# First attention of a fused kernel: block sums placed by one engine, keys and queries copied by ScalarE, the last two pairs' sums together, channel folds in another order

## The chip, the cores and the metric

One core of one Trainium2 chip runs the whole kernel. The metric is the device time of one execution in microseconds (us); lower is better. All data is float32 (the expert weights arrive as float64 and are converted on the chip).

## The reference

An attention with a local window and one summary key per block, then a Fourier mixing of tokens and channels with a two-layer network behind it.

```python
# attention: 4 batches, 8 heads, 768 tokens, head size 64; block 32, window 16
k_sum = k.reshape(B, H, nb, block, D).max(axis=3)
v_sum = v.reshape(B, H, nb, block, D).mean(axis=3)
scores_l = scale * q @ k.T          # kept where |i - j| < 16
scores_s = scale * q @ k_sum.T + log(block)
a = softmax(concat(scores_l masked, scores_s))
x = a @ concat(v, v_sum)            # heads side by side: (4, 768, 512)
# mixing and network
u = x + real(fft(fft(x, axis=1), axis=2))
un = (u - mean) / sqrt(var + 1e-6)
out = u + relu(un @ w_ch1) @ w_ch2  # 512 -> 2048 -> 512
```

## The kernel before

The batches run one behind the other: attention of the next batch beside the network of this one. Batch 0's attention stands alone at the start (`first_attention`); its order on TensorE (PE), VectorE (DVE) and ScalarE (ACT) is the order in which the code is written (`tc.manual_schedule`). All later instructions are placed by a scheduler, which also answers to code that changes ahead of them. SyncE issues the loads in program order, through eight completion lanes in turn.

The eight heads of batch 0 go as four pairs, g = 0 to 3. For a pair:

- `turn` transposes queries and keys on PE into PSUM (`qk`), four tiles a pair: keys or queries (n = 1 or 0), first or second head (e). `place` copies such a tile with two copies of 64x384 into `kt` or `qt` (L738). `key_maxima` takes the block maxima of the keys into `km` (L692, DVE).
- The scores come in two halves of the tokens: `wide_scores` (PE, L750 with the keys and L754 with the block maxima), `exponentials` (ACT, L759, one a head), `masks` (DVE, a product with `wide`, two a half).
- `add_parts` sums the pair's values by blocks on PE (L773, three parts in a group) into a PSUM bank `vs`, and ACT copies the sums to `words` (L776). `spread_sums` sends them through another matmul (L782), one a head, into the same bank; two copies then write them into rows 96 to 127 of the pair's values tile `vw` (L784): head 0 by DVE, head 1 by ACT, each 32x768.
- `wide_values` multiplies scores and values (PE, L792); DVE divides by the sums and writes the output block into `x`.

Round g works on pair g + 1's scores, places pair g's sums, turns pair g + 2's keys and queries, and ends with pair g's values. In the last round (n == NP) the last pair's own sums are made between its two halves of scores.

Behind each pair's values DVE folds tokens (`fold_sequence`: sums and differences of the two token halves, into `early`, the name `wide` in the profile), a pair's 128 channels at a time. Behind the attention `fold_halves` and `fold_ends` fold the channels into `fold`, for the two parities `par`. ACT writes some edge columns there (L985, L988, L992).

Then the scheduler's part begins: `add_later_blocks(1, 0)` (DVE sums of batch 1's values `vb`), the scaling of the loaded `half` into `vs` (L1822), the conversion of the weights (`convert`: L1145, L1158, L1161, L1163 on DVE, L1146 and L1159 on ACT), and the mixing (`gen_fourier`): matmuls `y` (L1307, L1311), ACT copies of them to `big` (L1312, L1313), matmuls `mx` (L1346, L1348), whose result DVE adds to `x`. Then come the normalisation and the first hidden layer (L1430).

Of the kernel before, what the change touches and what calls it, by code (L numbers as in the profile page):

```python
# [16 lines left out]
P = 128  # L17
# [479 lines left out]
def _main_program(ctx, tc, q, k, v, moe_w_ch1, moe_w_ch2, out):  # L497


    nc = tc.nc  # L500
    B, H, S, D = q.shape
# [79 lines left out]
    def tt(out, in0, in1, op):  # L581
        return nc.vector.tensor_tensor(out=out, in0=in0, in1=in1, op=op).ins  # L582
# [70 lines left out]
    def wide_vw(g):  # L653
        return (vw_bufs + [third, vw_bufs[0]])[g].rearrange("p (e n) d -> p e n d", e=2)
# [85 lines left out]
    def score_banks(g, half):  # L740
        return [abank([P, S2], f"sc_0_{g}_{half}_{e}") for e in range(2)]
# [14 lines left out]
    def exponentials(p, half, banks):  # L756
        n0, n1 = NQ // 2 * half, NQ // 2 * (half + 1)
        for e in range(2):
            nc.scalar.activation(out=p[:, e, n0:n1], in_=banks[e][:, 0:S2].rearrange("p (n c) -> p n c", c=QB), func=AF.Exp,  # L759
                                 scale=SC)  # L760

    def masks(p, half):
        n0, n1 = NQ // 2 * half, NQ // 2 * (half + 1)
        for e in range(2):
            tt(p[:, e, n0:n1], p[:, e, n0:n1], wide[:, None, :].to_broadcast([P, NQ // 2, QB]), ALU.mult)

    def add_parts(g):

        both = bank([P, 2, 2, D], f"vs_0_{g}")
        vw, ps = wide_vw(g), both[:, 0]  # L770
        for i in range(3):
            for c in range(4):
                nc.tensor.matmul(ps[32 * c:32 * (c + 1)], blk[0:WK, i], vw[0:WK, :, 3 * c + i, 0:D],  # L773
                                 start=i == 0, stop=i == 2)
        sums_of = words[:, 4096 + 2 * D * g:4096 + 2 * D * (g + 1)].rearrange("p (e d) -> p e d", e=2)
        nc.scalar.copy(out=sums_of, in_=ps)  # L776
        return sums_of, [both[WK - 32 * e:P - 32 * e, 1, 0] for e in range(2)]

    def spread_sums(g, sums_of, ps):

        for e in range(2):
            nc.tensor.matmul(ps[e], blk[:, 3], sums_of[:, e], start=True, stop=True)  # L782
        for e in range(2):
            (nc.scalar.copy if e else nc.vector.tensor_copy)(  # L784
                out=wide_vw(g)[WK:P, e, :, 0:D], in_=ps[e][:, None].to_broadcast([P - WK, NQ, D]))

    def wide_values(b, g, p, x):
        vw = wide_vw(g)
# [77 lines left out]
    def first_attention():  # L866

        x = x_of[0] = bpool.tile([P, NST, DM], FP, tag="x", bufs=2, name="x_0")
        fold = bpool.tile([P, 7, 2, S2], FP, tag="u", name="fold_0").rearrange("p a k n -> p (a k n)")
        wt["fold"] = split_fold(0, fold)  # L870
        turned = turned_to(0)
        for n in (1, 0):
            for e in range(2):
                turn(0, turned[0], n, e)
        for n in (1, 0):
            place(turned, n, 0, nc.scalar.copy)
            place(turned, n, 1, nc.vector.tensor_copy)
        key_maxima(0)
        load(0, 2)
        load_values(0, 1)  # L880
        load(0, 3)
        load_values(0, 2)
        ps, spread = {}, {}
        for g in range(-1, NP - 1):
            a, n = g + 1, g + 2
            first, second = score_banks(a, 0), None
# [19 lines left out]
            if n < NP:  # L906
                turn(n, turned[0], 0, 1)
                if g < 0:
                    place(turned, 0, 0, nc.scalar.copy)
                place(turned, 0, 1, nc.vector.tensor_copy)  # L910
            exponentials(ps[a], 1, second)
            if n < NP and g >= 0:
                place(turned, 0, 0, nc.scalar.copy)
            masks(ps[a], 1)
# [21 lines left out]
        keep_busy(3, ps[NP - 1][:, 0].rearrange("p n c -> p (n c)"))  # L936
        for par in range(2):
# [7 lines left out]
    def fold_sequence(par, g):  # L945

        x, c = x_of[0], slice(P * g, P * (g + 1))
        tt(early[par][:, :, c], x[:, 0:HT, c], x[:, HT:NST, c], SUB if par else ADD)

    def fold_halves(par, g):  # L950

        sd, zw = early[par], wt["fold"][:, par]
        lo, hi = slice(P * g, P * (g + 1)), slice(HD + P * g, HD + P * (g + 1))
        tt(zw[:, :, lo], sd[:, :, lo], sd[:, :, hi], ADD)
        tt(zw[:, :, hi], sd[:, :, lo], sd[:, :, hi], SUB)

    zqs, fgs = {}, {}

# [857 lines left out]
    weights = gen_weights()  # L1816
    with tc.manual_schedule(engines={mybir.EngineType.PE, mybir.EngineType.DVE, mybir.EngineType.Activation}):
        first_attention()
    add_later_blocks(1, 0)
    with tc.issue_after(marks["fold", 0]):  # L1820
        nc.vector.memset(vs, 0.0)
        nc.vector.tensor_scalar(out=vs[:, :, D], in0=half_of, scalar1=float(BLOCK), scalar2=None, op0=ALU.mult)  # L1822

# [92 lines left out]
```

## Time and profile before

| | us |
|---|---|
| median of 3 runs | 798.8 (797.18 to 800.85) |
| the profiled execution | 798.54 |
| its span, first to last instruction | 796.7 |
| PE busy, share of the span | 773.2, 97% |
| DVE busy | 539.1, 68% |
| ACT busy | 246.4, 31% |
| GpSimd busy | 75.1, 9% |

Shares are means over stages with different limits. The chain that ended last is 84% PE, 10% DVE and 4% ACT over the whole span, yet in the first 110 us it changes engine nearly every microsecond, so that stage is read instruction by instruction. In a timeline row stand the start, the duration, the engine, the line, the operation with what it writes and reads, the shape, the number of merged instructions, and in brackets the engine's idle time before it with what ended it. In a row of windows stand the window, then busy time and instructions of PE, its weight loads, DVE, ACT and POOL, the granted TensorE clock, the share of the DMA engines' time and GB/s.

### The profile page before, as it was taken

The numbers are of one execution on the slowest core, as the hardware profiler recorded it, in microseconds if no ns is written. First come the engines' busy times: TensorE is split into PE (matmuls) and PEld (weight loads), VectorE is DVE, ScalarE is ACT, GpSimd is POOL, SyncE is SP. The second block draws the span as 40 slices with busy tenths as digits, with TensorE's granted clock in tenths as the row PEclk, the third lists the DMA queues.
The fourth block names the chain that finished last, engine by engine and source line by source line (L and its number), as shares of the span: only waits on it lengthen the run. The fifth ranks groups of instructions, "written<-read, shape, count | busy, mean of one in ns | idle before, by whom it ended". The sixth has DMA issues, their size and how long they took to land.

```text
span 796.7 us, 14870 instructions
## 1 busy us (share of the span) xinstructions
PE 773.2 (97%) x6028; PEld 581.4 (73%) x6028; DVE 539.1 (68%) x1125; ACT 246.4 (31%) x573; POOL 75.1 (9%) x100
## 2 busy tenths in 40 slices
PE   8899979999999999999999999999999999999997
PEld 5578535545569876688669875688659889889986
DVE  4689999676878838564476726574376887756762
ACT  4545746524635212200126211310125214203300
POOL 0000000000000002200130002300040004201500
PEclk9989999999999999999999999999999999999999
DMA  9997598694774258995344049820614035204001
GB/s 192 262 238 154 133 303 219 213 297 129 212 214 140 78 159 182 254 174 133 119 179 156 31 144 210 218 97 27 250 46 154 29 123 209 93 1 185 1 28 56
DMA packets 135900, 120.35 MB, mean 151 GB/s; under 512 B 94512, under 2 KB 117392, under 8 KB 135824
## 3 DMA queue, kind: packets, MB, share of 16 engines
q1 hardware_dynamic: 134672, 117.05, 53.6%
q0 software_dynamic: 576, 2.10, 0.7%
q8 instruction: 49, 0.80, 0.5%
q10 hardware_dynamic: 576, 0.17, 0.1%
q14 instruction: 27, 0.22, 0.1%
HBM read 95.71 MB, written 23.59 MB: 150 GB/s over the span
## 4 chain that ended last, share of the span: by engine, by line
PE 84%; DVE 10%; ACT 4%; DMA 1%; issue 1%; POOL 0%; SPq 0%; DVEq 0%; ACTq 0%; POOLq 0%
PE ox L1723 17%; PE hx L1430 13%; PE oz L1723 9%; PE hz L1430 7%; PE o L1700 5%; PE oy L1723 4%; PE t L1603 4%; PE hy L1430 4%; PE y L1307 3%; PE f L1603 2%; PE mx L1266 2%; PE sc L808 2%; PE av L844 1%; PE av L849 1%; PE g L1603 1%
## 5 line engine op out<-in xcount | busy, mean ns | idle before, releaser
L1430 PE MATMUL hx<-u,w 128*128 128x384 f32 x384 | 141.1, 495 | 3.3 <-ACT h L1447 1.9
L1430 PEld LDWEIGHTS hx<-u,w 128*128 128x128 f32 x384 | 71.2, 191 | 57.5 <-ACT h L1447 4.4
L1723 PE MATMUL oz<-w,s 128*128 128x256 f32 x336 | 81.7, 380 | 0.0
L1723 PE MATMUL ox<-w,s 128*128 128x256 f32 x336 | 80.1, 380 | 0.0
L1723 PE MATMUL ox<-w,h 128*128 128x256 f32 x336 | 79.6, 381 | 0.0
L1723 PEld LDWEIGHTS ox<-w,h 128*128 128x128 f32 x336 | 63.0, 190 | 10.7 <-issue 1.2
L1430 PE MATMUL hz<-u,w 128*128 128x384 f32 x192 | 70.3, 489 | 0.5 <-DVE u L582 0.5
L582 DVE TENSOR_TENSOR x<-ox,x 128x256 f32<-128x256 f32 x84 | 35.5, 423 | 51.2 <-PE ox L1723 50.8
L1723 PEld LDWEIGHTS oz<-w,s 128*128 128x128 f32 x336 | 63.3, 190 | 8.9 <-DVE x L582 0.4
L1723 PEld LDWEIGHTS ox<-w,s 128*128 128x128 f32 x336 | 63.0, 190 | 9.2 <-DVE x L582 0.3
L1430 PEld LDWEIGHTS hz<-u,w 128*128 128x128 f32 x192 | 36.1, 190 | 26.5 <-DVE u L582 1.1
L1441 ACT COPY h<-hx 128x384 f32<-128x384 f32 x24 | 11.5, 478 | 123.1 <-PE hx L1430 123.1
L1700 PE MATMUL o<-w,h 128*128 128x512 f32 x96 | 41.9, 594 | 0.0
L1723 PE MATMUL oy<-w,h 128*128 128x256 f32 x168 | 40.6, 381 | 0.7 <-ACT h L1652 0.7
L1606 ACT COPY f<-t 128x192 f32<-128x192 f32 x52 | 15.8, 303 | 78.3 <-PE t L1603 78.1
L1582 POOL TENSOR_SCALAR h<-h 128x768 f32<-128x768 f32 x12 | 25.4, 2128 | 137.5 <-DVE h L1562 137.5
L585 POOL TENSOR_TENSOR vb<-vb 96x512 f32<-96x512 f32 (+2 forms) x20 | 20.7, 1037 | 179.0 <-DMA vb<-in_v_dram 112.6
L1430 PE MATMUL hy<-u,w 128*128 128x384 f32 x96 | 36.1, 496 | 0.9 <-DVE h L582 0.9
L1723 PEld LDWEIGHTS oy<-w,h 128*128 128x128 f32 x168 | 31.5, 190 | 5.9 <-ACT h L1652 1.5
L582 DVE TENSOR_TENSOR x<-oz,x 128x256 f32<-128x256 f32 x42 | 17.8, 423 | 26.7 <-PE oz L1723 26.4
L1700 PEld LDWEIGHTS o<-w,h 128*128 128x128 f32 x96 | 18.1, 190 | 22.5 <-issue 22.2
L1460 ACT ACTIVATE h<-hx 128x384 f32<-128x384 f32 x24 | 11.7, 489 | 62.7 <-PE hx L1430 62.7
(234 smaller groups left out, 1337.9 us busy)
## 6 DMA issues: line engine op xcount, KB each, us to landing
w<-dw SPq DMA_DIRECT2D x42, 896.0 KB, 5.9
words<-in_moe_w_ch_dram SPq DMA_DIRECT2D x32, 512.0 KB, 5.7
dw<-w SPq DMA_DIRECT2D x12, 896.0 KB, 6.9
vw<-in_v_dram SPq DMA_DIRECT2D x47, 192.0 KB, 6.1
out_dram<-x SPq DMA_DIRECT2D x23, 256.0 KB, 2.0
vb<-in_v_dram SPq DMA_DIRECT2D x24, 192.0 KB, 7.2
kn<-in_k_dram SPq DMA_DIRECT2D x9, 384.0 KB, 4.5
qn<-in_q_dram SPq DMA_DIRECT2D x9, 384.0 KB, 5.2
```

Of the source, the lines that this page charges most:

```text
L582: return nc.vector.tensor_tensor(out=out, in0=in0, in1=in1, op=op).ins
L585: return nc.gpsimd.tensor_tensor(out=out, in0=in0, in1=in1, op=op).ins
L808: ins = nc.tensor.matmul(ps[h][r:r + 64, i, :], kt[rows, o:o + 64], qt[rows, o:o + BLOCK], start=True, stop=True)
L1266: nc.tensor.matmul(out, y[:, g], table, start=False, stop=True, skip_group_check=True)
L1307: nc.tensor.matmul(y, fgs[b][par][:, st, P * g:P * (g + 1)], fs[par][:, g % 2, st, :], start=(st == 0), stop=(st == n - 1))
L1430: ins = nc.tensor.matmul(ps, w[:, a, kk, :], u[:, r, kk, :], start=start and kk == 0, stop=stop and kk == 1, skip_group_check=True)
L1460: nc.scalar.activation(out=c21, in_=X, func=AF.Relu)
L1582: nc.gpsimd.tensor_scalar(out=t, in0=t, scalar1=0.0, scalar2=None, op0=ALU.max)
L1603: marks["two"] = nc.tensor.matmul(o, left(j, a, m), rhs(r, m), start=m in (1, 5), stop=m in (2, 3, 4, 5, 7), skip_group_check=True).ins
L1606: nc.scalar.copy(out={1: f[:, 0], 6: f[:, 1], 7: g}[m], in_=t)
L1700: nc.tensor.matmul(ps, h[:, n, hf, P * t:P * (t + 1)], wt[2, b, j][:, 2 * hf:2 * hf + 2, :], start=(n, hf) == (0, 0), stop=(n, hf) == (NC ...
L1723: nc.tensor.matmul(ps, left[a][:, n, :], wt[2, b, j][:, r, :], start=start and n == 0, stop=stop and n == NC - 1, skip_group_check=True)
```

## The change

It does four things in `first_attention` and what it calls.

- A pair's sums go through one matmul of 128 columns instead of two of 64, and one copy (32 rows of 1536) places both heads: by DVE for the first three pairs, by ACT for the last. It stands ahead of the masks of the first half, where it stood behind them.
- For the first turned pair (g < 0) all four transposes come ahead of the second scores, and DVE copies the second head's keys and queries. From then on ACT makes all four copies; the last one and its transpose stand behind the second half's masks.
- In the last round both pairs' sums are made ahead of the scores and spread together.
- Tokens are folded two pairs at a time, 256 channels (`fold_sequence` with a range), once in round 1 and once behind the attention. `fold_channels` takes the place of `fold_halves` and of `fold_ends` for batch 0: the sums of the channel halves and all that needs them first, then the differences. `add_later_blocks(1, 0)` is now issued behind the last of it.

```diff
     def spread_sums(g, copy, sums_of, ps):
-        for e in range(2):
-            nc.tensor.matmul(ps[e], blk[:, 3], sums_of[:, e], start=True, stop=True)
-        for e in range(2):
-            (nc.scalar.copy if e else nc.vector.tensor_copy)(
-                out=wide_vw(g)[WK:P, e, :, 0:D], in_=ps[e][:, None].to_broadcast([P - WK, NQ, D]))
+        nc.tensor.matmul(ps, blk[:, 3], sums_of, start=True, stop=True)
+        copy(out=wide_vw(g)[WK:P, :, :, 0:D], in_=ps[:, :, None].to_broadcast([P - WK, 2, NQ, D]))
...
-            if g >= 0:
-                spread[g] = add_parts(g)
+            for i in (g, n - 1)[g < 0:1 + ends]:
+                spread[i] = add_parts(i)
             wide_scores(a, 0, first)
             exponentials(ps[a], 0, first)
+            if g >= 0:
+                spread_sums(g, nc.vector.tensor_copy, *spread[g])
+            if ends:
+                spread_sums(n - 1, nc.scalar.copy, *spread[n - 1])
             masks(ps[a], 0)
-            if g >= 0:
-                spread_sums(g, *spread[g])
             second = score_banks(a, 1)
-            if n < NP:
+            if not ends:
                 turned = turned_to(n)
-                for i in ((1, 0), (1, 1), (0, 0)):
+                for i in ((1, 0), (1, 1), (0, 0), (0, 1))[:3 + (g < 0)]:
                     turn(n, turned[0], *i)
                 place(turned, 1, 0, nc.scalar.copy)
-                place(turned, 1, 1, nc.scalar.copy)
+                place(turned, 1, 1, nc.vector.tensor_copy if g < 0 else nc.scalar.copy)
+                place(turned, 0, 0, nc.scalar.copy)
+                if g < 0:
+                    place(turned, 0, 1, nc.vector.tensor_copy)
                 key_maxima(n % 2)
-            else:
-                spread[n - 1] = add_parts(n - 1)
             wide_scores(a, 1, second)
...
             exponentials(ps[a], 1, second)
-            if n < NP and g >= 0:
-                place(turned, 0, 0, nc.scalar.copy)
             masks(ps[a], 1)
-            if n == NP:
-                spread_sums(n - 1, *spread[n - 1])
+            if g >= 0 and not ends:
+                turn(n, turned[0], 0, 1)
+                place(turned, 0, 1, nc.scalar.copy)
...
-            for par in range(2 if g >= 0 else 0):
-                fold_sequence(par, g)
-        fold_halves(0, 0)
+            for par in range(2 if g == 1 else 0):
+                fold_sequence(par, 0, 2)
...
         for par in range(2):
-            fold_sequence(par, NP - 1)
-            if par:
-                fold_halves(par, 0)
-            fold_halves(par, 1)
-            for _ in fold_ends(0, par, wt["fold"][:, par], wt["fold"][:, 2 - 2 * par]):
-                pass
+            fold_sequence(par, 2, NP)
+            fold_channels(par)
...
+    def fold_channels(par):
+        Q = DM // 4
+        sd, zw, fg = early[par], wt["fold"][:, par], wt["fold"][:, 2 - 2 * par]
+        tt(zw[:, :, 0:HD], sd[:, :, 0:HD], sd[:, :, HD:DM], ADD)
+        nc.scalar.copy(out=fg[:, :, 0:1], in_=zw[:, :, 0:1])
+        tt(fg[:, :, 1:Q], zw[:, :, 1:Q], zw[:, :, HD - 1:Q:-1], ADD)
+        nc.scalar.copy(out=zqs[0][:, par, :, 0], in_=zw[:, :, Q])
+        nc.vector.memset(fg[:, :, Q:Q + 1], 0.0)
+        tt(fg[:, :, Q + 1:HD], zw[:, :, 1:Q], zw[:, :, HD - 1:Q:-1], SUB)
+        tt(zw[:, :, HD:DM], sd[:, :, 0:HD], sd[:, :, HD:DM], SUB)
+        nc.scalar.copy(out=fg[:, :, HD:HD + 1], in_=zw[:, :, HD:HD + 1])
+        nc.scalar.copy(out=fg[:, :, DM - 1:DM], in_=zw[:, :, HD + Q:HD + Q + 1])
+        tt(fg[:, :, HD + 1:HD + Q], zw[:, :, HD + 1:HD + Q], zw[:, :, DM - 1:HD + Q:-1], SUB)
+        marks["fold", 0] = tt(fg[:, :, HD + Q:DM - 1], zw[:, :, HD + 1:HD + Q], zw[:, :, DM - 1:HD + Q:-1], ADD)
...
-    add_later_blocks(1, 0)
     with tc.issue_after(marks["fold", 0]):
+        add_later_blocks(1, 0)
         nc.vector.memset(vs, 0.0)
```

What stands on the engines, at the places that matter. In the names the first numbers are batch, pair, and half or head; the last is a running number. ScalarE in the round of pair 2's scores, before:

```order
L759 ACTIVATE p_0_2_416<-sc_0_2_0_0_414 128x384
L759 ACTIVATE p_0_2_416<-sc_0_2_0_1_415 128x384
L784 COPY vw1_85<-vs_0_1_417 32x12x64
L738 COPY kt1_81<-qk_0_3_1_0_456 64x384 x2
L738 COPY kt1_81<-qk_0_3_1_1_460 64x384 x2
L759 ACTIVATE p_0_2_416<-sc_0_2_1_0_453 128x384
L759 ACTIVATE p_0_2_416<-sc_0_2_1_1_454 128x384
L738 COPY qt_0_3_455<-qk_0_3_0_0_464 64x384 x2
L776 COPY words_103<-vs_0_2_534 128x128
```

and now:

```order
L759 ACTIVATE p_0_2_412<-sc_0_2_0_0_410 128x384
L759 ACTIVATE p_0_2_412<-sc_0_2_0_1_411 128x384
L738 COPY kt1_81<-qk_0_3_1_0_450 64x384 x2
L738 COPY kt1_81<-qk_0_3_1_1_454 64x384 x2
L738 COPY qt_0_3_449<-qk_0_3_0_0_458 64x384 x2
L759 ACTIVATE p_0_2_412<-sc_0_2_1_0_447 128x384
L759 ACTIVATE p_0_2_412<-sc_0_2_1_1_448 128x384
L738 COPY qt_0_3_449<-qk_0_3_0_1_487 64x384 x2
L776 COPY words_103<-vs_0_2_528 128x128
```

The copy into `vw1` is gone from ScalarE, the first query copies stand ahead of the second exponentials, and the second ones, which VectorE made, behind them.

VectorE behind the folds, before:

```order
L642 TENSOR_REDUCE vbs_1_0_393<-vb_1_0_0_394 96x64
L1145 TENSOR_SCALAR words_103<-words_103 128x1024
L1158 TENSOR_SCALAR w1_0_0_755<-words_103 128x1024
L1822 TENSOR_SCALAR vs_86<-half_76 128x2
L1161 SCALAR_TENSOR_TENSOR words_103<-words_103 128x1024
L1163 SCALAR_TENSOR_TENSOR w1_0_0_755<-words_103,w1_0_0_755 128x1024
L582 TENSOR_TENSOR x_0_145<-mx_0_0_818,x_0_145 128x2x256
```

and now:

```order
L642 TENSOR_REDUCE vbs_1_0_391<-vb_1_0_0_392 96x64
L1822 TENSOR_SCALAR vs_86<-half_76 128x2
L1145 TENSOR_SCALAR words_103<-words_103 128x1024
L1158 TENSOR_SCALAR w1_0_0_741<-words_103 128x1024
L1161 SCALAR_TENSOR_TENSOR words_103<-words_103 128x1024
L1163 SCALAR_TENSOR_TENSOR w1_0_0_741<-words_103,w1_0_0_741 128x1024
L582 TENSOR_TENSOR x_0_145<-mx_0_0_804,x_0_145 128x2x256
```

The row that reads `half`, a small table that SyncE loads, moved from behind the conversion's first two rows to ahead of them.

More of the change, by code (lines that the diff above doesn't have):

```diff
@@ L776, in add_parts, with spread_sums @@
         nc.scalar.copy(out=sums_of, in_=ps)
-        return sums_of, [both[WK - 32 * e:P - 32 * e, 1, 0] for e in range(2)]
-    def spread_sums(g, sums_of, ps):
-        for e in range(2):
-            nc.tensor.matmul(ps[e], blk[:, 3], sums_of[:, e], start=True, stop=True)
-        for e in range(2):
-            (nc.scalar.copy if e else nc.vector.tensor_copy)(
-                out=wide_vw(g)[WK:P, e, :, 0:D], in_=ps[e][:, None].to_broadcast([P - WK, NQ, D]))
+        return sums_of, both[WK:P, 1]
+    def spread_sums(g, copy, sums_of, ps):
+        nc.tensor.matmul(ps, blk[:, 3], sums_of, start=True, stop=True)
+        copy(out=wide_vw(g)[WK:P, :, :, 0:D], in_=ps[:, :, None].to_broadcast([P - WK, 2, NQ, D]))
     def wide_values(b, g, p, x):
@@ L936, in first_attention, with fold_sequence @@
         keep_busy(3, ps[NP - 1][:, 0].rearrange("p n c -> p (n c)"))
+        nc.gpsimd.memset(zqs[0], 0.0)
         for par in range(2):
[L938 to L955 removed]
+            fold_sequence(par, 2, NP)
+            fold_channels(par)
+    def fold_sequence(par, g0, g1):
+        x, c = x_of[0], slice(P * g0, P * g1)
+        tt(early[par][:, :, c], x[:, 0:HT, c], x[:, HT:NST, c], SUB if par else ADD)
+    def fold_channels(par):
[12 more added lines that the diff above has]
+        marks["fold", 0] = tt(fg[:, :, HD + Q:DM - 1], zw[:, :, HD + 1:HD + Q], zw[:, :, DM - 1:HD + Q:-1], ADD)
     zqs, fgs = {}, {}
```

11 lines of the change are left out of this document (4 added, 7 removed).

## The prediction

> **What bounds the kernel now.** I read the windows first, then the chain of waits, then the timeline engine by engine for the first 70 us, since everything that changes lies there. Times are us from the span's start. From 38 to 44.8 us TensorE is busy throughout, but at a granted clock of 0.50 (the column behind POOL), and the DMA engines are full (1.08, the next):
>
> ```profile
> 38.00:44.80 6.80, 6.80 (x75) 4.21 (x73) 4.14 (x9) 2.80 (x6) 0.00 (x0) 0.50 1.08 303
> ```
>
> The first attention goes pair by pair. On TensorE a round starts with the scores (L750), which waited 0.95 us for the placed queries, and the sum scores (L754):
>
> ```profile
> 15.98 1.23 PE L750 MATMUL sc<-qt,kt 64*96 64x64 f32 x22 [0.40 <-DVE qt L738]
> 25.33 1.65 PE L750 MATMUL sc<-qt,kt 64*96 64x64 f32 x24 [0.95 <-ACT qt L738]
> 26.91 0.83 PE L754 MATMUL sc<-qt,km 64*32 64x384 f32 x4
> 29.05 1.24 PE L750 MATMUL sc<-qt,kt 64*96 64x64 f32 x24
> 30.22 0.83 PE L754 MATMUL sc<-qt,km 64*32 64x384 f32 x4
> 35.98 1.65 PE L750 MATMUL sc<-qt,kt 64*96 64x64 f32 x24 [0.95 <-ACT qt L738]
> ```
>
> So pair 1's round took 25.33 - 15.98 = 9.35 us and pair 2's 10.65. What fills a round stands on ScalarE and VectorE:
>
> ```profile
> 27.78 0.88 ACT L759 ACTIVATE p<-sc 128x384 f32<-128x384 f32 x2 [2.21 <-PE sc L754]
> 31.24 0.79 ACT L784 COPY vw<-vs 32x768 f32<-32x768 f32 x1 [2.58 <-DVE vw L784]
> 32.05 2.11 ACT L738 COPY kt<-qk 64x384 f32<-64x384 f32 x4
> 34.19 0.87 ACT L759 ACTIVATE p<-sc 128x384 f32<-128x384 f32 x2
> 34.95 0.99 ACT L738 COPY qt<-qk 64x384 f32<-64x384 f32 x2
> 28.25 1.03 DVE L582 TENSOR_TENSOR wide<-x 128x384 f32<-128x384 f32 x2
> 30.24 0.96 DVE L784 COPY vw<-vs 32x768 f32<-32x768 f32 x1
> 35.16 1.13 DVE L738 COPY qt<-qk 64x384 f32<-64x384 f32 x2
> ```
>
> ScalarE idles 2.58 us until VectorE has placed its half of the block sums (30.24 + 0.96 = 31.20), and the key copies queue behind. That wait sets the round, while TensorE's 0.95 us is only its tail. After the attention VectorE sets the end: last output block at 50.78, folds until 58.99, then the value sums, the weight conversion from 62.73, the mixing's additions from 67.73.
>
> ```profile
> 44.41 1.03 DVE L582 TENSOR_TENSOR p<-p,wide 128x384 f32<-128x384 f32 x2 [2.55 <-ACT p L759]
> 50.78 0.56 DVE L582 TENSOR_TENSOR x<-av,rec 128x384 f32<-128x384 f32 x1
> 55.25 1.96 DVE L582 TENSOR_TENSOR fold<-wide 128x384 f32<-128x384 f32 x4
> 58.99 1.29 DVE L582 TENSOR_TENSOR vb<-vb,vb 96x512 f32<-96x512 f32 x2
> 62.73 0.68 DVE L1145 TENSOR_SCALAR words<-words 128x1024 int32<-128x1024 int32 x1
> 63.93 0.16 DVE L1822 TENSOR_SCALAR vs<-half 128x2 f32<-128x2 f32 x1
> 67.73 0.68 DVE L582 TENSOR_TENSOR x<-mx,x 128x512 f32<-128x512 f32 x1
> 68.34 1.22 DVE L582 TENSOR_TENSOR w<-w,words 128x1024 f32<-128x1024 f32 x1
> ```
>
> **Part 1, one copy places a pair's sums.** The ScalarE copy (0.79) and its wait go. VectorE copies 1536 instead of 768 elements a partition. No row shows that size. Below, it costs the 0.96 of the half; above, twice that, 1.92. Two query copies of 384 take 1.13, so 0.56 for 384 and 0.96 for 768 are 0.40 per 384; I take 0.96 + 0.80 = 1.76, nearest to the large form. On ScalarE (0.53 for 384 from the four key copies, 0.79 for 768) the same step gives 1.3. Serial halves (0.96 + 0.79 = 1.75) and one whole of 1.76 are the same to the values matmul; the gain is that ScalarE is free.
>
> A rule against it: the Trainium skill, "PSUM — Partial Sum Buffer", Specifications (TRN2), says that ScalarE and VectorE can access PSUM in parallel at full rate where no bank collides. By it the two halves would finish together and this edit would lengthen the placement by 0.8 us a pair. Here the halves ran one behind the other, 0.04 us apart; both lie in one bank.
>
> **Part 2, keys and queries on ScalarE.** From pair 2 on, VectorE loses a query copy of 1.13 a pair and ScalarE gains one of 0.99; it also comes after the second exponentials. The new round is ScalarE's: scores until the first exponentials 27.78 - 25.33 = 2.45, these until the next row 34.95 - 34.19 = 0.76, key copies 2.13, queries 1.0, exponentials 0.76, queries 1.0: 8.1 us. TensorE's second scores and sums (30.22 + 0.83 = 31.05, that is 5.7 into the round) are done before ScalarE comes to them at 6.3, and VectorE's share, the wide copy and four masks (two take 1.03) with the maxima and two outputs, stays below it. Against 10.65 pair 2's round wins 2.55, against 9.35 pair 1's wins 1.25. For pair 1 the second key half and the queries now stand on VectorE ahead of the maxima, so the scores at 15.98 come earlier by something between the 0.40 that they waited and the 1.13 of a query copy: 0.75, the middle. Together 4.55; pair 3's scores start at 35.98 - 4.55 = 31.4. Bounds of the part: 2.0 (the ScalarE copy of 0.79 in each of two rounds, and the 0.40) to 4.9 (with 1.13).
>
> **Part 3, the last two pairs' sums together.** The last pair's summing (1.50) moves from between its score halves to before them, where TensorE waited 0.95 for the queries anyway:
>
> ```profile
> 38.82 1.50 PE L773 MATMUL vs<-vw,wide 96*32 96x128 f32 x22
> 40.25 2.19 PE L750 MATMUL sc<-qt,kt 64*96 64x64 f32 x24
> 42.37 1.49 PE L754 MATMUL sc<-qt,km 64*32 64x384 f32 x4
> 47.36 1.62 PE L792 MATMUL av<-vw,p 128*64 128x65 f32 x46 [0.49 <-ACT vw L784]
> 45.47 0.96 DVE L784 COPY vw<-vs 32x768 f32<-32x768 f32 x1
> 46.52 0.79 ACT L784 COPY vw<-vs 32x768 f32<-32x768 f32 x1 [1.76 <-DVE vw L784]
> ```
>
> Its two serial copies (45.47 to 47.31) also stood between the last masks and the last values; now ScalarE's copy (1.3) lies beside the second scores. From 31.4: scores 1.65, sums 0.83, spread 0.35, second scores 1.24, sums 0.83, an exponential 0.48, masks 1.03 give 37.8, or 39.7 if these matmuls run at half clock as they did here (2.19 and 1.49). The last values end 1.7 us later (1.62 here), and the last output block 1.9 after that (here 51.34 - 48.98 = 2.36, with a fold of 0.47 in between): 41.4 to 43.3, against 50.78 + 0.56 = 51.34. That is 8.0 to 9.9 earlier. The pair's values must have landed:
>
> ```profile
> 23.92 4.15 SPq L562 DMA_DIRECT2D vw<-in_v_dram  x6
> vw<-in_v_dram SPq DMA_DIRECT2D x4, 20.0 KB, 2.9
> 48.52 0.43 SPq L562 DMA_DIRECT2D half<-c_half  x1
> half<-c_half SPq DMA_DIRECT2D x1, 1.0 KB, 7.7
> DMA  9979982399988999999999999999999999999879
> ```
>
> The last of the six is issued by 27.7 and such loads land 2.9 later, at 30.6; TensorE comes to it at about 30 (31.4 less the pairs' two sums). A wait of up to 0.6 lies beside the wait for the queries.
>
> **Part 4, the folds.** Folding moves out of the rounds (the two of 1.03 at 28.25 go) to fewer, wider instructions, partly behind the last block. Four of 384 take 1.96, 0.47 apart; 512 takes 0.68 and 1024 takes 1.22, so 768 some 0.95, or 0.87 apart. Behind the last block VectorE needed 58.99 - 51.34 = 7.65; now three of 0.87 and four of 0.47 a parity, 4.5, twice, 9.0. This gives back 1.35. The small edge copies on ScalarE, eight instead of six, lie beside it. The folds end at 50.4 to 52.3: 6.7 to 8.6 earlier, in the middle 7.65.
>
> **Part 5, what VectorE meets next.** In the new order the scaling of `half` (L1822) stands ahead of the first conversion (L1145), which it followed before. VectorE comes to it 62.73 - 58.99 = 3.74 after the folds, at 54.1 to 56.0. But `half` lands at 48.52 + 7.7 = 56.2, and that does not move: from 30 us the DMA engines are full in nearly all slices (the last row: 23 to 57 us in 40 slices), and SyncE's order is unchanged until long after (GpSimd's throughout). So VectorE waits 0.2 to 2.1 us, with the conversion behind it; ScalarE's exponent step behind that; and behind it, on ScalarE, the last mixing copies for which TensorE waits:
>
> ```profile
> 63.60 0.82 PE L1307 MATMUL y<-fs,fold 128*128 128x193 f32 x4
> 64.01 1.17 ACT L1146 ACTIVATE words<-words,rebias 128x1024 int32<-128x1024 int32 x1
> 65.44 0.70 PE L1348 MATMUL mx<-fd,big 128*128 128x256 f32 x2 [1.03 <-ACT big L1312]
> ```
>
> L1145 runs at 56.4, L1146 at 57.1 instead of 64.01 (it was ready at 62.73 + 0.68 = 63.41, and ScalarE held by the transform's copies). What follows keeps its distance from it: the mixing resumes at 58.5 and VectorE's additions start at 60.8, 6.9 us earlier. The cap (6.9) and the middle of the attention's gain (7.65) nearly meet.
>
> **Part 6, behind it.** From there to 250 us a few conversion and hidden-layer instructions change places. No row prices that; each is 0.2 to 1.3 us and as often earlier as later: 0, bounds -1.5 to +1.5.
>
> For TensorE's clock I subtract half of one halved window. After an idle stretch the trace shows the clock at 0.50:
>
> ```profile
> 108.14 0.80 PE L844 MATMUL av<-vw,p 64*32 64x65 f32 x50 [3.39 <-issue]
> 109.70:113.00 3.30, 3.11 (x5) 1.83 (x6) 2.08 (x5) 2.60 (x4) 0.00 (x0) 0.50 1.05 359
> ```
>
> The first transform now ends 5.4 after the folds (64.42 - 58.99), at 55.8 to 57.7, so TensorE idles 0.8 to 2.7 us until 58.5, less than that 3.39. A halved stretch of 3.4 us would cost 1.7, with a chance of one half 0.9. The Trainium skill, "TensorE: Matmul & The Clock Gate", What's actually happening, has the clock halve after an idle window of about 3.4 us. At 109.7 the trace agrees; the halved stretch from 38 us, with waits like the 0.95 at 35.98 ahead of it, does not.
>
> Sum: 6.9 - 0.9 = 6.0. The profiled execution took 798.54 (span 796.7 and 1.84 around it); the median of three is 798.8. Forecast: 792.5.
>
> **Rivals.** *`half` does not bind*, because it lands some 2 us earlier: with the folds done at 50.4 the attention's gain holds in full, 8.6 us, 790.0. The full DMA slices speak against it.
>
> *The rounds do not shrink* to 8.1, another wait taking the place (a PSUM bank for the fourth transpose, or the wide VectorE copy ahead of the masks): part 2 gives 2.0 instead of 4.55, so 2.55 of the 7.65 go and the cap is out of reach: 5.1 less 0.9 is 4.2, 794.3; with no shrinking at all 796.3. VectorE's idle 2.55 at 44.41 speaks for room.
>
> *The clock halves in the dense mixing.* Two stretches like the 6.8 from 38.0 cost 3.4 each where TensorE sets the end: 6.9 - 6.8 leaves nothing, 798.4.
>
> *Slower: the load of `half`.* The one place where VectorE, ScalarE and TensorE now all queue behind a transfer is L1822. Each us that it lands after 56.2 is lost. From 63.1 there is no gain, and beyond 67 the kernel is slower by over 0.5%; at 68, 803.4. Landings that keep within the full slices of the row above speak against it.
>
> **How the numbers follow.** Forecast 0.55 (790.5 to 794.8), no binding 0.13, rounds 0.18, clock 0.10, `half` late 0.04. The range runs from 788.5 (the attention's 9.9) to 797.0, which leaves out most of the clock case and the slow one. A measurement of this kernel tells 0.5%, 4 us, from no change, so faster means below 794.8: forecast, no binding and a third of the rounds, less the edge, 0.70; the same 0.25; slower 0.05.
>
> **What would show it.** Right: in the new profile no ScalarE wait on L784's successor, rounds near 8.1, folds ending at 50 to 52, VectorE idle just before L1822 until 56.2, mixing from 58.5. Wrong: key copies that still start over 3 us after the first exponentials; VectorE busy through L1822; a clock of 0.50 between 58 and 72; the 6 us at 70 us missing at 250.

## The result, and the profile after

The changed kernel takes 793.3 us (median, 790.9 to 798.6) against 799.4 (797.2 to 800.9) in the same comparison: a ratio of 0.9931, 95% interval 0.9903 to 0.996. The profiled execution took 792.55 us with a span of 790.8, against 798.54 and 796.7: 6.0 less, as forecast. How the 6.0 came about is another matter, and most of this part is about that.

The two stretches below answer to the one at half clock that opened the prediction (window, PE, its weight loads, DVE, ACT, POOL, granted clock, DMA share, GB/s). The halved stretch at 38 us is gone. A new one of the same length, 6.83 us, starts at 101.17; before, one of 3.41 us stood at 109.67.

```profile
38.00:44.80 6.80, 6.51 (x75) 4.72 (x70) 6.53 (x15) 2.07 (x6) 0.14 (x1) 1.00 1.07 290
101.20:108.00 6.80, 5.72 (x31) 2.83 (x38) 4.59 (x8) 3.63 (x6) 0.00 (x0) 0.50 1.04 373
```

The timeline of the changed kernel, TensorE: the scores that open the rounds of pairs 1, 2 and 3, the last pair's sums, the last values.

```profile
14.64 1.24 PE L750 MATMUL sc<-qt,kt 64*96 64x64 f32 x24
22.85 1.24 PE L750 MATMUL sc<-qt,kt 64*96 64x64 f32 x24
31.08 0.98 PE L773 MATMUL vs<-vw,wide 96*32 96x128 f32 x24
32.00 1.24 PE L750 MATMUL sc<-qt,kt 64*96 64x64 f32 x24
37.86 1.62 PE L789 MATMUL av<-vw,p 128*64 128x65 f32 x48
```

No row has a bracket: from 13 to 42 us TensorE waits for nothing. The rounds take 22.85 - 14.64 = 8.21 and 32.00 - 22.85 = 9.15 us and are TensorE's own work; the 0.9 us more in the second is the last pair's summing, which now stands bare ahead of the scores. ScalarE and VectorE in the same stretch:

```profile
24.88 0.87 ACT L759 ACTIVATE p<-sc 128x384 f32<-128x384 f32 x2 [1.60 <-PE sc L754]
25.75 2.08 ACT L738 COPY kt<-qk 64x384 f32<-64x384 f32 x4
25.22 1.76 DVE L782 COPY vw<-vs 32x1536 f32<-32x1536 f32 x1 [1.49 <-PE vs L781]
34.44 1.76 DVE L782 COPY wide<-vs 32x1536 f32<-32x1536 f32 x1 [0.61 <-PE vs L781]
34.92 1.43 ACT L782 COPY vw<-vs 32x1536 f32<-32x1536 f32 x1
40.54 0.56 DVE L582 TENSOR_TENSOR x<-av,rec 128x384 f32<-128x384 f32 x1
```

ScalarE goes from the exponentials straight to the keys, where it idled 2.58 us; the wide copy takes 1.76. Folds and what stands behind the attention (the folds end where the `vb` row starts, 50.85):

```profile
32.00 1.82 DVE L582 TENSOR_TENSOR wide<-x 128x768 f32<-128x768 f32 x2
41.13 0.96 DVE L582 TENSOR_TENSOR wide<-x 128x768 f32<-128x768 f32 x1
42.13 0.96 DVE L582 TENSOR_TENSOR fold<-wide 128x768 f32<-128x768 f32 x1
50.85 1.28 DVE L582 TENSOR_TENSOR vb<-vb,vb 96x512 f32<-96x512 f32 x2
54.81 0.17 DVE L1822 TENSOR_SCALAR vs<-half 128x2 f32<-128x2 f32 x1 [0.15 <-DMA half<-c_half]
54.89 0.69 DVE L1145 TENSOR_SCALAR words<-words 128x1024 int32<-128x1024 int32 x1
55.77 1.19 ACT L1146 ACTIVATE words<-words,rebias 128x1024 int32<-128x1024 int32 x1
57.23 0.70 PE L1348 MATMUL mx<-fd,big 128*128 128x256 f32 x2 [1.05 <-ACT big L1312]
59.52 0.68 DVE L582 TENSOR_TENSOR x<-mx,x 128x512 f32<-128x512 f32 x1
```

In this execution `half` landed at 54.79, and VectorE waited only 0.15 for it. The first addition of the mixing comes 67.73 - 59.52 = 8.21 earlier than before. TensorE keeps this lead until 100 us (its row at 99.92 stood at 108.14 before: 8.22). Behind the longer halved window 7.07 is left (126.42 against 133.49), and then it shrinks here:

```profile
127.00 0.69 DVE L1145 TENSOR_SCALAR words<-words 128x1024 int32<-128x1024 int32 x1 [1.38 <-DMA words<-in_moe_w_ch_dram]
128.74 0.55 DVE L582 TENSOR_TENSOR h<-hx,h 128x384 f32<-128x384 f32 x1
129.35 1.56 PE L1430 MATMUL hx<-u,w 128*128 128x384 f32 x4 [1.48 <-DVE h L582]
```

A conversion waits for its weights with the addition of a hidden piece queued behind it, and TensorE waits for that addition. Before, no such wait stood there. The output layer (L1700) starts at 137.44 instead of 143.13, 5.7 earlier.

### The profile page after: what moved, and what is told of

It reads as the page before. It is cut to its first block, busy times and chain, and to the rows that moved or that the text cites. A ratio compares the mean times of both kernels' runs of the same rounds, so it can differ in the third digit from the quotient of the medians.

```text
span 790.8 us, 14849 instructions
## 1 busy us (share of the span) xinstructions
PE 768.1 (97%) x6020; PEld 578.5 (73%) x6020; DVE 537.7 (68%) x1114; ACT 246.4 (31%) x574; POOL 75.0 (9%) x100
## 4 chain that ended last, share of the span: by engine, by line
PE 84%; DVE 9%; ACT 2%; DMA 2%; issue 1%; SPq 1%; DVEq 0%; ACTq 0%
PE ox L1723 17%; PE hx L1430 13%; PE oz L1723 9%; PE hz L1430 6%; PE o L1700 5%; PE oy L1723 4%; PE t L1603 4%; PE hy L1430 3%; PE y L1307 3%; PE f L1603 2%; PE mx L1266 2%; PE sc L805 2%; PE av L841 2%; PE av L846 1%; PE g L1603 1%; PE unt L1402 1%
## 5 line engine op out<-in xcount | busy, mean ns | idle before, releaser
L1700 PE MATMUL o<-w,h 128*128 128x512 f32 x96 | 41.9, 594 | 0.0
L1700 PEld LDWEIGHTS o<-w,h 128*128 128x128 f32 x96 | 18.1, 190 | 22.5 <-issue 21.7
L582 DVE TENSOR_TENSOR h<-hy,h 128x384 f32<-128x384 f32 x24 | 13.3, 556 | 27.0 <-PE hy L1430 26.9
```

Source lines behind the costliest of these rows:

```text
L1700: nc.tensor.matmul(ps, h[:, n, hf, P * t:P * (t + 1)], wt[2, b, j][:, 2 * hf:2 * hf + 2, :], start=(n, hf) == (0, 0), stop=(n, hf) == (NC ...
```

## The experiments

The table puts all runs side by side: start of the scores of pairs 1, 2 and 3 (where two matmuls run ahead of a wait, the group behind it), end of the last output block, end of the folds, landing of `half`, and the mixing's first row behind its wait, all in us of the run's timeline; then the time from the second attention's first scores to the output layer, and the ratio to the kernel before in the same job. Starts differ between runs, where a halved window fell into the first 16 us (e3, e4, e5), so lengths are read as differences within a run.

| run | pair 1 | 2 | 3 | block | folds | half | mixing | to output | median us, ratio (95%) |
|---|---|---|---|---|---|---|---|---|---|
| before | 15.98 | 25.79 | 36.43 | 51.34 | 58.99 | 56.24 | 65.44 | 66.25 | 799.4, 1 |
| after | 14.64 | 22.85 | 32.00 | 41.10 | 50.85 | 54.79 | 57.23 | 68.77 | 793.3, .9931 (.9903 to .996) |
| e1 | 15.20 | 24.50 | 33.84 | 44.47 | 54.21 | 54.91 | 60.58 | 68.12 | 795.6, .9952 (.9937 to .9967) |
| e2 | 15.70 | 23.89 | 32.75 | 42.22 | 51.96 | 56.42 | 58.67 | 70.34 | 795.5, .9955 (.9941 to .9969) |
| e3 | 16.66 | 24.87 | 33.08 | 43.89 | 53.63 | 56.30 | 60.00 | 67.43 | 791.2, .9898 (.9884 to .9911) |
| e4 | 18.37 | 26.57 | 35.43 | 46.93 | 54.59 | 56.69 | 61.04 | 68.77 | 793.9, .9934 (.991 to .9958) |
| e5 | 16.59 | 24.79 | 33.66 | 42.93 | 52.67 | 55.38 | 59.03 | 67.12 | 792.7, .9912 (.9892 to .9933) |
| e6 | 14.68 | 22.88 | 31.75 | 40.85 | 50.60 | 31.99 | 56.95 | 68.69 | 791.5, .9899 (.9884 to .9913) |
| e7 | 14.68 | 22.88 | 31.75 | 40.84 | 50.58 | 56.49 | 58.74 | 79.39 | 804.4, 1.0052 (1.0037 to 1.0066) |
| e8 | 14.63 | 23.52 | 33.02 | 42.61 | 52.35 | 56.49 | 58.74 | 69.84 | 793.7, .992 (.9904 to .9936) |
| e9 | 15.50 | 23.70 | 31.90 | 43.63 | 51.29 | 54.96 | 57.74 | 67.15 | 792.4, .9919 (.9906 to .9931) |
| e10 | 14.68 | 22.88 | 31.75 | 40.85 | 50.60 | 57.14 | 59.39 | 69.02 | 793.7, .994 (.9923 to .9957) |
| e11 | 14.71 | 22.91 | 31.78 | 40.88 | 50.62 | 31.86 | 56.98 | 67.28 | 791.0, .9905 (.9891 to .992) |
| e12 | 14.90 | 23.11 | 31.97 | 41.06 | 50.80 | 31.71 | 57.16 | 67.62 | 791.0, .9905 (.9891 to .992) |

**e9, part 1 alone in the kernel before.** The copy as in the change (both hunks of `spread_sums`), placed ahead of the masks; nothing else.

```diff
+            if g >= 0:
+                spread_sums(g, nc.vector.tensor_copy, *spread[g])
             masks(ps[a], 0)
-            if g >= 0:
-                spread_sums(g, *spread[g])
...
-                spread_sums(n - 1, *spread[n - 1])
+                spread_sums(n - 1, nc.scalar.copy, *spread[n - 1])
```

> The kernel before with part 1 alone: one wide copy by VectorE ahead of the masks for the first three pairs, by ScalarE for the last, queries, last sums and folds as they were. Theory (the ScalarE half and its wait were what made the rounds 9.35 and 10.65; the rest of the change only trims the ends): rounds of 8.2 to 8.6, the last now VectorE's own (1.76 + 1.03 + 0.95 + 1.13 + 1.03 + 1.5 + 1.03 = 8.4 us of work a round), the last output block at 44.5 to 46.5 instead of 51.34, and most of the gain: 794 to 795.5. Rival (the prediction's accounting, which gives the copy alone the lower bound of 2.0 us and the rest to the queries and the last sums): 797.

Timeline of e9: scores, ScalarE, last output block, end of the folds.

```profile
23.70 1.24 PE L750 MATMUL sc<-qt,kt 64*96 64x64 f32 x24
23.86 0.27 ACT L776 COPY words<-vs 128x128 f32<-128x128 f32 x1 [1.15 <-PE vs L773]
31.90 1.24 PE L750 MATMUL sc<-qt,kt 64*96 64x64 f32 x24
43.08 0.56 DVE L582 TENSOR_TENSOR x<-av,rec 128x384 f32<-128x384 f32 x1
51.29 1.29 DVE L582 TENSOR_TENSOR vb<-vb,vb 96x512 f32<-96x512 f32 x2
```

Rounds of 8.2, with ScalarE now waiting for TensorE, and no halved window before 100 us. The folds end 7.70 us earlier than before; with all four parts they end 8.14 earlier. Counted from pair 1's scores it is 35.79 against 43.01 before and 36.21 with all four, so the others win only ahead of pair 1. Even the theory had expected too little (block at 44.5 to 46.5). The one copy is the whole change but for some 0.4 us at this point, and its time, 792.4, is no worse than that of the changed kernel in the same job (e10, 793.7; the intervals overlap). Part of these 7 us is the last round's, which holds the halved stretch at 38 us before; the record has one profile of the kernel before, so how often that stretch falls there is not known.

**e1, the copy undone in the change.** Two copies again, from one PSUM bank, for the first three pairs and the last.

```diff
-        copy(out=wide_vw(g)[WK:P, :, :, 0:D], in_=ps[:, :, None]...)
+        for e, half in enumerate((copy, nc.scalar.copy)):
+            half(out=wide_vw(g)[WK:P, e, :, 0:D], in_=ps[:, e][:, None]...)
```

> Theory (ScalarE's queue and TensorE's own work both fill a round, 8.2 us, with 0.24 us between them): a ScalarE copy of 0.79 per pair back ahead of the key copies lengthens the rounds by 0.55 to 0.8 each and the last one by 0.8, so the last output block ends 1.9 to 2.4 us later than 41.10, the mixing starts by as much later than 57.23, and the time is about 795.5. If VectorE's half and ScalarE's half run at the same time, VectorE's copy is 0.8 shorter; if ScalarE again waits for VectorE's half, the round grows by 0.85 to 1.1. Rival (TensorE alone sets the rounds, ScalarE has room): rounds stay 8.2, last block within 0.3 of 41.1, 793.3.

```profile
26.87 0.96 DVE L783 COPY vw<-vs 32x768 f32<-32x768 f32 x1 [1.25 <-PE vs L781]
27.87 0.79 ACT L783 COPY vw<-vs 32x768 f32<-32x768 f32 x1 [0.47 <-DVE vw L783]
```

Rounds of 9.30 and 9.34 (the second is hardly longer than the 9.15 with one copy, since the last pair's summing fills TensorE's wait; the last round is 10.63 instead of 9.10). ScalarE waits for VectorE's half again, and from pair 1's scores to the last block it takes 44.47 - 15.20 = 29.27 instead of 26.46: the theory, with the wait (0.47 + 0.79 a round).

**e8, two copies from two banks.** Why does ScalarE wait? Here head 1's sums get a bank of their own.

```diff
+        own = bank([P, D], f"vs1_0_{g}")[WK:P]
+        nc.tensor.matmul(own, blk[:, 3], sums_of[:, 1], start=True, stop=True)
+        nc.scalar.copy(out=wide_vw(g)[WK:P, 1, :, 0:D], in_=own[:, None]...)
```

> Part 1 in another form: two copies of 768, VectorE's and ScalarE's, each from a PSUM bank of its own. Theory (the two copies ran one behind the other because they read one bank, so that the program made ScalarE wait for VectorE's, and not because the engines cannot read at once): both start within 0.3 us of the sums' matmul or of ScalarE's exponentials, take 0.96 and 0.79 as alone, and overlap. ScalarE's queue is still 0.79 longer than with the one wide copy, so a round takes 8.7 to 8.9 instead of 8.2, against 9.3 with both copies from one bank; last block 1.2 to 1.8 later than in the changed kernel counted from pair 1's scores, time 794.5. Rival (they disturb each other): the overlapping copies take longer, in sum 1.75 as one behind the other, rounds 9.3, time 795.6.

```profile
25.78 0.96 DVE L784 COPY vw<-vs 32x768 f32<-32x768 f32 x1 [1.18 <-PE vs L782]
26.44 0.79 ACT L785 COPY vw<-vs 32x768 f32<-32x768 f32 x1
```

ScalarE no longer waits, the two overlap by 0.30 us, and each takes what it took alone. So the wait came with the shared bank, and the engines can read at once. (Head 1's sums have a tile of their own here too; whether tile or bank makes the program wait is not separated.) Still the round is longer (8.89 and 9.50) than with the wide copy, since ScalarE's queue is: 42.61 - 14.63 = 27.98 to the last block.

**e2, the query copies undone, the wide copy kept.**

```diff
-                for i in ((1, 0), (1, 1), (0, 0), (0, 1))[:3 + (g < 0)]:
+                for i in ((1, 0), (1, 1), (0, 0)):
...
+                if g < 0:
+                    place(turned, 0, 0, nc.scalar.copy)
+                place(turned, 0, 1, nc.vector.tensor_copy)
             exponentials(ps[a], 1, second)
+            if not ends and g >= 0:
+                place(turned, 0, 0, nc.scalar.copy)
```

> Part 2 alone undone, the one wide copy kept. Theory (with ScalarE free of its half of the sums, TensorE's own 8.2 us are the round, and ScalarE's last query copy only fills its slack): rounds stay at 8.2, and only the first turned pair is later again, its scores at 15.3 to 16.0 instead of 14.64; last block 0.7 to 1.4 later, about 794.4. Rival (the prediction's accounting, where moving the query copies is what brings the round from over 9 to 8.1): rounds of 9 to 9.4, last block 2.5 to 3.5 later, 796.

```profile
23.89 1.24 PE L750 MATMUL sc<-qt,kt 64*96 64x64 f32 x24
24.06 0.27 ACT L776 COPY words<-vs 128x128 f32<-128x128 f32 x1 [1.15 <-PE vs L773]
56.45 0.17 DVE L1823 TENSOR_SCALAR vs<-half 128x2 f32<-128x2 f32 x1 [0.68 <-DMA half<-c_half]
```

Rounds 8.2 and 8.86; from pair 1's scores to the last block 26.52 against 26.46. Where ScalarE has 1.15 us to spare, moving a copy to it wins nothing in the rounds. Only the first pair's scores come 1.06 later. In this run `half` landed at 56.42 and cost 0.68. Its time, 795.5, is worse by more than that: the stage to the output layer takes 70.34 instead of 68.77. TensorE's wait of 1.48 at 129.35 is 2.12 here, and a halved window stands behind it.

**e3, the last pair's sums apart again.**

```diff
-            for i in (g, n - 1)[g < 0:1 + ends]:
+            for i in (g,)[g < 0:]:
...
+            else:
+                spread[n - 1] = add_parts(n - 1)
...
+            if ends:
+                spread_sums(n - 1, nc.scalar.copy, *spread[n - 1])
```

> Part 3 alone undone: the last pair's sums again between its halves of scores. Theory (the second summing, 0.95 us of TensorE, lay bare ahead of the last scores, since no wait for the queries is left): pair 3's scores start at 31.05 instead of 32.00, but the sums' ScalarE copy of 1.43 now comes behind the second exponentials and the last values start at 38.3 instead of 37.86; the last block ends 0.3 to 0.8 us later than 41.10 and the time is 793.8. Rival (the prediction's accounting: 3.5 us and more of the gain are this part's): last block at 44.5 or later, 796.8.

```profile
33.08 1.24 PE L750 MATMUL sc<-qt,kt 64*96 64x64 f32 x24
40.74 1.73 PE L789 MATMUL av<-vw,p 128*64 128x65 f32 x48 [0.48 <-ACT vw L782]
```

From pair 1's scores to the last block 27.23 against 26.46: part 3 wins 0.8 at this point, not 3.5. Yet the kernel is not slower than the changed one: its ratio, 0.9898, lies below 0.9931 and 0.994 in the latter's two jobs, though the interval overlaps the first of these. Its order behind the attention is another, since the scheduler answers to the code ahead: the scaling of `half` stands behind the conversion, and the wait at 127 us is not there (67.43 to the output layer, where the changed kernel needs 68.77).

**e4, the folds of before in the changed attention.**

```diff
-            for par in range(2 if g == 1 else 0):
-                fold_sequence(par, 0, 2)
+            for par in range(2 if g >= 0 else 0):
+                fold_sequence(par, g, g + 1)
+        fold_halves(0, 0)
```

and behind the attention `fold_halves` and `fold_ends` as before.

> Part 4 alone undone: the folds of before, per pair in the rounds, behind the new attention. Theory: behind the last block the folds need 7.65 instead of 9.75 us and end at 48.8 to 49.3 instead of 50.85; VectorE then comes to the scaling of half at 52.7 and waits for its landing until 54.8, so the conversion runs at 54.9 as now and the mixing starts within 0.4 of 57.23: 793.3. Rival (half is no cap, and what the mixing waits for is the folds): the mixing starts 1.6 to 2.1 earlier, 791.4. Second rival (the extra folding slows the rounds, where VectorE is nearly full): last block 0.5 to 2 later, 794 to 795.

```profile
43.57 1.03 DVE L582 TENSOR_TENSOR wide<-x 128x384 f32<-128x384 f32 x2
46.37 0.56 DVE L582 TENSOR_TENSOR x<-av,rec 128x384 f32<-128x384 f32 x1
```

The second rival held. Behind the last block the folds take 7.66 instead of 9.75, but folding between the output blocks makes the last round 11.50 instead of 9.10 us. From pair 1's scores to the folds' end it is 36.22 against 36.21: the reorder is worth nothing either way.

**e6, `half` early; e10, the changed kernel again.**

```diff
+                fetch(out=half_of, in_=dr["half"].ap())
                 load(1, 0)
...
-                fetch(out=half_of, in_=dr["half"].ap())
                 fetch(out=mirror, in_=dr["mirror"].ap())
```

> The changed kernel with the load of half issued 20 us earlier, its scaling one row earlier on VectorE; TensorE's and ScalarE's order are the same. Theory (VectorE waited 0.15 for half in the changed kernel's profile, and ScalarE came to the exponent step only 0.19 after its input was ready): the wait goes and the mixing starts within 0.2 of where it did, counted from the end of the folds (6.92 us behind it); time 793.3. Rival (the prediction's cap, half landing at 56.2 or later in most executions): 1 us or more is won in most of them, about 792. This run also tells the changed kernel's time anew.

> The changed kernel once more, beside the others of this job, for the landing of half and the halved windows of another execution. Theory (half binds in the executions where it lands at 56 or later, and costs 1 to 2 us there): where it lands at 56.5, VectorE waits some 2 us ahead of the scaling and the mixing starts 9 us behind the folds instead of 6.9; time 792 to 794. Rival: the mixing starts 6.9 us behind the folds whatever half does.

First e10, then e6: the scaling on VectorE and the mixing's first row behind its wait on TensorE, and a window of e10.

```profile
57.16 0.17 DVE L1822 TENSOR_SCALAR vs<-half 128x2 f32<-128x2 f32 x1 [2.76 <-DMA half<-c_half]
59.39 0.70 PE L1348 MATMUL mx<-fd,big 128*128 128x256 f32 x2 [3.46 <-ACT big L1312]
60.20:63.60 3.40, 3.40 (x10) 2.69 (x9) 3.14 (x4) 0.30 (x1) 0.00 (x0) 0.50 1.19 213
```

```profile
52.52 0.16 DVE L1822 TENSOR_SCALAR vs<-half 128x2 f32<-128x2 f32 x1
56.95 0.70 PE L1348 MATMUL mx<-fd,big 128*128 128x256 f32 x2 [1.03 <-ACT big L1312]
```

In e10 the same program's `half` landed at 57.14. VectorE waited 2.76 us, TensorE 3.46, and TensorE's clock was halved for 3.41 us behind that: the mixing starts 8.79 us behind the folds instead of 6.38. With `half` early it is 6.35. So the theory of e6 (half hardly matters), read from one profile, was wrong, and the prediction's cap is real: it depends on the landing, which lay between 54.8 and 57.1 in the eleven profiles with the load in its old place (median 56.3), mostly because the loads ahead of it shift: SyncE issued `half` at 47.32 in the changed kernel's first profile and at 49.31 in e10. e6's median of 791.5 came in another job than the control's 793.7; the intervals of their ratios do not overlap, though e6's overlaps that of the changed kernel's first comparison.

**e5, the additions ahead of the conversion.** One conversion's first step is issued a step later.

```diff
-        if m < 2:
+        if m < 2 or m == 7:
             exponents(m)
...
-        if 0 < m < NIT - 1:
+        if 0 < m < NIT - 1 and m != 6:
             exponents(m + 1)
```

> The changed kernel with one conversion (the one that follows the third piece of the second weights) started one step later, so that on VectorE the additions of the third hidden piece, for which TensorE waits, stand ahead of it and not behind it. Theory (of the 8.2 us at 70 us about 1.4 are lost again there: VectorE idles 1.38 at 127.00 for the weights' load with those additions queued behind, and TensorE idles 1.48 at 129.35 for them): TensorE's idle time there goes, the first output matmul comes 68.2 us after the first score of the second attention or sooner instead of 68.8 us, and the time is 1.2 to 1.5 less, about 792. Rival (that stage is bound by the load however the rows stand, or what is won there is lost at the next wait before 140 us): the time within 0.4 of the changed kernel's 793.3.

```profile
127.13 0.55 DVE L582 TENSOR_TENSOR h<-hx,h 128x384 f32<-128x384 f32 x1
128.73 0.55 DVE L582 TENSOR_TENSOR h<-hz,h 128x384 f32<-128x384 f32 x1
129.20 0.69 DVE L1145 TENSOR_SCALAR words<-words 128x1024 int32<-128x1024 int32 x1
```

The waits on both engines are gone, and the stage takes 67.12 instead of 68.77: 1.65 less, as expected there. In the median of the times (792.7) it cannot be told from the changed kernel. Nor does e11 tell it: with `half` early in both, that stage takes 67.28 in e11 and 68.69 in e6, but their ratios, 0.9905 and 0.9899, are alike.

**e7 and e12, filling TensorE's idle stretch.** Matmuls ahead of the second attention's second values, 96 of them on top of e5 and 10 on top of e11.

```diff
+        for _ in range(96 if (b, g) == (1, 1) else 0):
+            nc.tensor.matmul(av[0][:, 0, :], ident, ident[:, 0:D1], start=True, stop=True)
```

> As the run with the additions first, and 96 small matmuls more in TensorE's queue where it idled 3.4 us at 96.5; the order of the rows behind changes with them. Their result is overwritten. Theory (the clock halves because of that idle stretch, at the next boundary of its 3.41 us windows, and stays halved until a window without idle time): no window of 0.50 between 98 and 110, and the matmuls from 102 to 108 take 1 us less; how much of it reaches the end is open, since VectorE is busy throughout from 80 to 104: 0 to 1. Rival (the halving does not come from idling): the window of 0.50 stays.

> As the run before this one, with 10 matmuls more in the idle stretch of TensorE at 96.5 (0.20 us each, as the 96 took 19.5 us), all other rows in the same order. Their result is overwritten. Theory (the halved window follows from a window with more than about 2 us of idle time): of the 3.4 us idle 1.4 stay, the window of 0.50 after 100 goes or is 3.41 instead of 6.83 us long, and the matmuls behind it take up to 1 us less: 0.5 to 1 below the run before. Rival (the stage is VectorE's, or the rest of the idling still halves the clock): no difference.

First e7's window, then e12's wait and window.

```profile
96.00:110.00 14.00, 14.00 (x128) 14.00 (x127) 11.47 (x17) 4.60 (x7) 0.00 (x0) 1.00 1.02 319
```

```profile
100.45 1.16 PE L843 MATMUL av<-vw,p 64*32 64x65 f32 x66 [2.60 <-DVE p L582]
100.70:107.50 6.80, 5.56 (x73) 3.19 (x50) 5.16 (x9) 2.79 (x5) 0.00 (x0) 0.50 1.04 372
```

Without the idle stretch there is no halved window, but 96 were far too many (0.2 us each): the stage became 10.6 us longer, and the kernel slower than before. Ten shortened the wait only from 3.39 to 2.60; the halving stayed, and the time is that of e11. That the halving at this place comes with the idling is shown; how much idling it takes, and what a fill of the right size would win, is not.

**e11, `half` early and the additions first** (the edits of e6 and e5 together).

> The changed kernel with half loaded early and with the additions ahead of the conversion. Theory: both gains add, 0.5 to 1.5 for half (in the mean of its landings) and 1.4 for the additions: 2 to 3 below the changed kernel of the same job, about 790. Rival (one wait only takes the place of the other): no more than 1.5 below it.

791.0 against 793.7 of the control, ratios 0.9905 (0.9891 to 0.992) and 0.994 (0.9923 to 0.9957): the two waits that the change had brought cost 2.7 us together. How this splits between them is open, since e6 alone does as well. The ratios of e3, e5, e6, e9 and e12 lie within its interval. So no run shows that parts 2 to 4 win anything on top of the copy in the time of the kernel.

## Why the prediction was right, point by point

**The number** (792.5 against 793.3) and the sign held, with the mechanism at the head of it: ScalarE's half and its wait set the rounds. But several terms were mis-sized, and the errors cancelled, so that the number came so close is in part luck.

**Part 1.** The wide copy was forecast at 1.76 and took 1.76; ScalarE's at 1.3 took 1.43. The step that failed is the lower bound of 2.0 us at pair 3's scores (in part 2), which is what the copy alone was given: it counted ScalarE's two copies of 0.79 and a wait of 0.40, and left out that the wait of 2.58 for VectorE's masks and copy goes with them. Alone the copy takes the two rounds from 36.43 - 15.98 = 20.45 to 31.90 - 15.50 = 16.40, 4.05 less (e9). The rule of the Trainium skill that was weighed against the row, "PSUM — Partial Sum Buffer", Specifications (TRN2), is borne out by e8: from two banks the halves ran at once. The row of before (ScalarE's 2.58 for VectorE's copy) showed a wait that the program makes.

**Part 2.** Rounds of 8.1 were forecast, 8.2 came, but for the wrong reason: not ScalarE's queue sets them, TensorE's own work does, and moving the queries gave nothing beyond the first pair (1.06, e2; forecast 0.75). TensorE's busy time over pair 1's round before (8.62 of the 9.81 us from 15.98 to 25.79) would have shown that its own work is as long as ScalarE's new queue.

**Part 3.** The block was forecast at 41.4 to 43.3 and ended at 41.10, the full-clock case. The step that failed is that the summing moves to "where TensorE waited 0.95 for the queries anyway": there is no such wait any more, and the second summing lay bare for 0.9 (rows at 31.08 and 32.00). The part is worth 0.8 at the last block (e3). The rest of the last round's gain came with the copy: e9's takes 11.73 instead of 14.91, without a halved window. Two sums of the prediction are slightly off: with the two rows that it names the half-clock case gives 39.4 and not 39.7, and 798.54 less 9.9 is 788.6.

**Part 4.** Forecast: 9.0 behind the block, 1.35 given back. It took 9.75, because instructions of 768 that need each other's result follow each other at 0.99 to 1.00 (rows at 41.13 and 42.13); the 0.87 of the forecast holds for two that do not (1.82 for both at 32.00, of 0.95 each). What the old folds would have cost inside a faster last round (2.4) was not counted; the balance is 0 (e4).

**Part 5.** "That does not move", of `half`'s landing, was the weak step. The landing moves by 2.3 us from one execution to the next. In the profile it was 54.79 and the cap 8.2 instead of 6.9; in e10 57.14, with the first addition only 6.05 earlier. The forecast of 6.9 lies between these.

**Part 6 and the clock.** The reorder was put at 0 with bounds of 1.5; undone at one place it gives 1.65 in its stage (e5), just beyond the bound. No halved window came at 58 us in the profile, but one did in e7 and e10, where `half` was late; what it cost there was not measured apart. The longer halved window at 101 us, over which the lead falls from 8.22 to 7.07, was not in the sum. The 6.0 at 70 us are 6.0 at the end by way of 8.2 and 2.2 lost.

Of the rivals, "the rounds do not shrink" is refuted, "half does not bind" and the cap are both true, each in some executions. The dense mixing did not run at half clock in the changed kernel's profile (1.00 from 58 to 72 us); in e10 and e7 it did for one window, and no run shows the two long stretches of the rival.

## What to carry to other kernels

Look first for an engine that stands in a queue for another's half of the same job: give the whole job to one of them, even if it takes twice as long there. Before pricing what else moves, sum the rows of each engine over one round; the largest sum is the floor, and edits below it win nothing. When a stage comes 8 us earlier, list the transfers that were just in time, and look at what is queued behind the instruction that waits for each: here two such rows gave back 2.7 us.

## What the runs showed of the hardware

- A copy's duration grew with the elements of a partition, also for 32 partitions read with a broadcast: on VectorE 0.96 for 768 and 1.76 for 1536, on ScalarE 0.79 and 1.43.
- The halved windows start on one grid within an execution: before at 37.99, 109.67 and 113.08 (its end), 21 and 1 times 3.413 us apart. A window that was idle for 2.5 of its 3.41 us came ahead of one of them (after: 97.76 to 101.17), and the halving held through a second window, the first of the two having 1.1 us idle. The Trainium skill, "TensorE: Matmul & The Clock Gate", What's actually happening, gives a free-running window of 3413 ns, which agrees, and an idle window as the cause, where less than a whole one did it here.
- No rule by the idle share of one window comes out of these traces. Before, TensorE was busy for 2.39 of the 3.41 us from 34.58 to 37.99, and the clock was 0.50 behind that; from 102.84 to 106.26 it was busy for only 1.56 and the clock stayed at 1.00. The window from 37.99 to 41.40 was busy throughout, and the next was halved as well. What started the stretch at 38 us stays open.
- The landing of one load, issued at the same place of one program, differed by 2.35 us between two executions (the changed kernel: 54.79 and 57.14).
